# Gate logits and routing of a fused spectral-filter and mixture-of-experts kernel: transposes on VectorE in 32x32 blocks in place of TensorE's, and routing in a swapped order of columns

## The chip, the core and the metric

The kernel runs on one core of one Trainium2 chip. Its time is what the device needs for one execution, in microseconds (us). All arithmetic is in fp32. The engines are TensorE (PE in the profile, with PEld for its loads of the stationary operand), VectorE (DVE), ScalarE (ACT), GpSimd (POOL) and SyncE (SP, which issues most transfers). Each engine works its own instructions off in order and waits on semaphores for the others.

## The reference

Eight batches of 2496 tokens with 256 channels are filtered in the frequency domain along the tokens. Each filtered token then goes to the one of eight experts with the largest gate logit: two matrices, a relu between them, and the result times the softmax weight of that expert.

```
X = np.fft.rfft(x, axis=1)                    # x: (8, 2496, 256)
y = np.fft.irfft(X * (filt_r + 1j * filt_i), n=2496, axis=1)
y = y.reshape(19968, 256)
logits = y @ w_gate                           # (19968, 8)
expert_idx = argmax(logits); gate_w = softmax(logits)[expert_idx]
out = gate_w * (relu(y @ w1[e]) @ w2[e])      # w1: (8, 256, 1024), w2: (8, 1024, 256)
```

## The kernel before

**The filter.** A batch of 2496 = 39 x 64 tokens is transformed by matrix products in four stages, `stage_a` to `stage_d` (L342 to L412). Stages a and b are the forward transform over 39 and over 64 points, stages c and d go back. Between a and b, and between c and d, the data goes through DRAM (`zd`, `ud`) and comes back in another layout; the first batch stays in the chip and is turned by transposes on TensorE instead. `stage_d` writes y into tiles `yo`, 117 tokens (three groups of 39) to a partition column: 22 columns a batch, in six chunks of at most four, `CH`. Each chunk's `yo` is one of six buffers (`YB`).

**The logits.** `turn_y` transposes a chunk on TensorE against the identity, 117x128 at a time, so that the channels lie on the partitions (L482), and copies the result from PSUM to the tile `yt` (four buffers). `logits` multiplies `yt` by the gate matrix, two halves of 128 channels, with four column tiles of 32 side by side (L496); `ls` takes the result out of PSUM. `turn_logits` transposes it back on TensorE (L507) and copies it to `lgs`, so that tokens lie on partitions again. Every such copy goes through `evac`, whose line in the profile is L234 and which gives it to DVE or ACT by the planner's own count of how busy they are.

**The routing.** `route` (L514 to L599) handles a group of two chunks, up to eight columns: DVE finds the largest logit and the expert. Two matmuls count the tokens ahead of each one within its expert (L554 with the triangle `tri`, L555 with `ones`), a scan adds the counts of earlier columns, and out comes the row that each token takes in the list of its expert. GpSimd writes the token's number and weight behind its 256 channels and scatters the rows to DRAM, one column of 117 rows to an instruction (L615). Only when a chunk's rows are scattered may its `yo` be written again.

**The experts.** Tiles of 512, 256 or 128 rows of one expert are read back, transposed on DVE (L748) and go through the first matrix (L791 for most tiles, with seven products of quarters in place of eight; L832 for the others), the relu, and the second (L849). The results are scattered to the output (L855).

**The order.** PE, DVE, ACT and SP follow an order that is written by a planner while the program is built. `slot(k)` lists the steps of batch k's middle stages, of the next batch's first and of the previous batch's last stage with its logits and routing, each with a place in the slot and a cost in us of TensorE time. A running clock `now` adds these costs; expert steps are put between the filter steps as soon as the planner believes that their rows and weights are there. Instructions of `route` are handed out a few at a time after each step, from a list `sides` of which only the first entry moves.

Of the kernel before, what the change touches and what calls it, by code (L numbers as in the profile page):

```python
# [19 lines left out]
P = 128  # L20
S = 2496
D = 256
# [16 lines left out]
FT = F // P  # L39

# [13 lines left out]
def dft_tables():  # L54

    w = 2.0 * np.pi  # L60
    q = np.arange(N1)
    t = np.arange(N2)

    ta = np.zeros((NB, N1, NB, NS))
    td = np.zeros((NB, NS, NB, N1))
    for f in range(NF):
        ang = w * ((q * f) % N1) / N1
        for j in range(NB):
            ta[j, :, j, f] = np.cos(ang)
            td[j, f, j] = (2.0 if f else 1.0) / S * np.cos(ang)  # L70
            if f:
                ta[j, :, j, NF + f] = -np.sin(ang)
                td[j, NF + f, j] = -2.0 / S * np.sin(ang)

    ang = w * ((t[:, None] * t[None, :]) % N2) / N2
    c, sn = np.cos(ang), np.sin(ang)
    tb = np.block([[c, -sn], [sn, c]])
    tc = np.block([[c, sn], [-sn, c]])

    ids = np.zeros((NB, N1, NG))  # L80
    valid = np.zeros((NB, N1, NG))
    for j in range(NB):
        for i in range(len(range(j, N2, NB))):
            ids[j, :, i] = token(q, NB * i + j)
            valid[j, :, i] = 1.0


    sg = np.where(coefficients() <= S // 2, 1.0, -1.0)

    return {  # L90
        "ta": ta.reshape(TP, TK),
        "tb": tb,
        "tc": tc,
        "td": td.reshape(TK, TP),
        "sg": np.concatenate([sg[:, :NF // 2], sg[:, NF // 2:]]),
        "ids": ids.reshape(TP, NG),
        "valid": valid.reshape(TP, NG),
    }
# [22 lines left out]
def kernel(  # L121
# [65 lines left out]
    tds = cst.tile([TK, TP], F32, name="tds")  # L187
# [4 lines left out]
    CT = 32  # L192
    wg = cst.tile([P, DH, CT], F32, name="wg")
    tri = cst.tile([TP, TP], F32, name="tri")
    ones = cst.tile([TP, P], F32, name="ones")

    WM = 8
# [4 lines left out]
    vld = cst.tile([TP, NG], F32, name="vld")  # L202
# [63 lines left out]
    def load_rest():  # L266
        nc.sync.dma_start(out=tds, in_=td)
        nc.vector.memset(wg, 0.0)
        nc.sync.dma_start(out=wg[:, :, :E], in_=moe_w_gate.rearrange("(i p) e -> p i e", p=P))
        nc.sync.dma_start(out=ids0, in_=ids)  # L270
        nc.sync.dma_start(out=vld, in_=valid)

    def make_constants():
        make_identity(nc, ident)
        nc.gpsimd.memset(ones, 1.0)
        nc.gpsimd.affine_select(
            out=tri, in_=ones[:, :TP], compare_op=ALU.is_gt, fill=0.0, base=0, pattern=[[1, TP]], channel_multiplier=-1
        )
        nc.gpsimd.memset(seg, 1.0)
        nc.gpsimd.memset(seg[:, :, 0:1], 0.0)  # L280
        nc.gpsimd.memset(tot, 0.0)
        nc.gpsimd.iota(prow, pattern=[[0, 1]], base=0, channel_multiplier=1)
        nc.gpsimd.iota(tau_i, pattern=[[1, 64]], base=0, channel_multiplier=0)
        nc.vector.tensor_copy(tau0, tau_i)
        nc.gpsimd.iota(e_i, pattern=[[1, E]], base=0, channel_multiplier=0)
        nc.vector.tensor_scalar(em8, in0=e_i, scalar1=-float(E), scalar2=None, op0=ALU.add)
        nc.vector.tensor_scalar(eoff, in0=e_i, scalar1=float(TE), scalar2=None, op0=ALU.mult)
        nc.vector.tensor_copy(cnt, eoff)
        nc.vector.tensor_copy(done, eoff[0:1, :])
        nc.vector.memset(one, 1.0)  # L290
# [10 lines left out]
    ins, outs, lgs, yts, lands = {}, {}, {}, {}, {}  # L301
# [95 lines left out]
    def stage_d(b, c):  # L397
        if c == 0:
            lgs[b] = sb.tile([TP, NG, E], F32, tag="lg", name="lg")
# [3 lines left out]
        yo = outs["o", b, c] = sb.tile([P, 4, DR], F32, tag="y", name="yo", bufs=YB)[:TP]  # L403
        for j in range(0, n, 2):
            p = bank()
            if i0 + j + 2 < NG:
                mm(p[:TP, :], lhsT=tds, rhs=ui[:TK, j:j + 2, :], start=True, stop=True)
            else:

                for i, k in enumerate((TK, NS)):  # L410
                    mm(p[:TP, i * D:(i + 1) * D], lhsT=tds[:k, :], rhs=ui[:k, j + i, :], start=True, stop=True)
            evac(yo[:, j:j + 2, :D], p[:TP, :].rearrange("p (i d) -> p i d", i=2), 512)  # L412
# [63 lines left out]
    def turn_y(b, c):  # L476
        yo = outs["o", b, c]
        for j in range(0, CH[c][1], 2):
            pt = bank().rearrange("p (i q) -> p i q", i=4)
            for i in range(2):  # L480
                for dh in range(DH):
                    nc.tensor.transpose(  # L482
                        pt[:, 2 * i + dh, :TP], yo[:, j + i, dh * P:(dh + 1) * P], ident[:TP, :TP]
                    )
            yt = yts[b, c, j] = sb.tile([P, 4, TP], F32, tag="yt", name="yt", bufs=4)
            evac(yt, pt[:, :, :TP], 4 * TP)

    def logits(b, g):

        js = range(min(4, NG // 2 - 4 * g))  # L490
        w = len(js) * CT
        pair = [yts.pop((b, 2 * g + j // 2, 2 * (j % 2))).rearrange("p (i h) q -> p i h q", i=2) for j in js]
        lt = psr.tile([P, 2, E * NG], F32, tag="lt", name="lt")[:, :, :TP]
        for dh in range(DH):
            for j in js:
                mm(lt[j * CT:(j + 1) * CT], lhsT=wg[:, dh, :], rhs=pair[j][:, :, dh, :],  # L496
                   start=(dh == 0), stop=(dh == DH - 1))
        ls = sb.tile([P, 2, TP], F32, tag="ls", name="ls", bufs=1)
        evac(ls[:w], lt[:w], 2 * TP)
        outs["l", b] = (g, w, ls)  # L500

    def turn_logits(b):
        g, w, ls = outs.pop(("l", b))
        n = w // CT
        pt = bank()[:TP, :2 * w].rearrange("p (i w) -> p i w", i=2)
        for i in range(2):
            nc.tensor.transpose(pt[:, i, :], ls[:w, i, :], ident[:w, :w])  # L507
        evac(lgs[b][:, 8 * g:8 * g + 2 * n, :].rearrange("p (j i) e -> p i j e", i=2),
             pt.rearrange("p i (j c) -> p i j c", c=CT)[:, :, :, :E], 16 * n)

# [3 lines left out]
    def route(b, c0, c1):  # L514

        t0 = 4 * c0
        w = min(4 * c1, NG) - t0
        lg = lgs[b][:, t0:t0 + w]
        sh3 = (TP, w, E)
        she = (TP, E, w)  # L520

        def small(name, *shape, dt=F32, tag=None):
            n = int(np.prod(shape))
            full = sb.tile([TP, WM * n // w], dt, tag=tag or name, name=name, bufs=1)[:, :n]
# [10 lines left out]
        nc.vector.tensor_tensor(oh, oh, em8[:TP, None, :].to_broadcast(sh3), op=ALU.mult)  # L535
# [3 lines left out]
        if t0 + w == NG:  # L539

            nc.vector.tensor_tensor(idx, idx, vld[:, t0:t0 + w], op=ALU.mult)
        oe = small("oe", E, w)
        nc.vector.tensor_tensor(
            oe, idx[:, None, :].to_broadcast(she), em8[:TP, :, None].to_broadcast(she), op=ALU.is_equal
# [9 lines left out]
        mm(rk[:TP, 0, :E * w], lhsT=tri, rhs=oef, start=True, stop=True)  # L554
        mm(rk[:, 1, :E * w], lhsT=ones, rhs=oef, start=True, stop=True)  # L555
        pos = small("pos", E, w, tag="oh")
        nc.scalar.copy(out=pos.rearrange("p e t -> p (e t)"), in_=rk[:TP, 0, :E * w])
# [3 lines left out]
        sd = small("sd", w)  # L561
# [7 lines left out]
        nc.vector.tensor_tensor(pos, pos, tot[:TP, :, :w], op=ALU.add)  # L569
        yield 2  # L570
        nc.vector.tensor_tensor(pos, pos, oe, op=ALU.mult)
        row = sb.tile([TP, WM], U32, tag="row", name="row", bufs=2)[:, :w]
        rowf = small("rowf", w)
        nc.vector.tensor_reduce(rowf, pos.rearrange("p e t -> p t e"), axis=AX.X, op=ALU.add)
        yield 2
        nc.vector.tensor_copy(row, rowf)
        nc.vector.tensor_copy(cnt, tot[:, :, w])
        yield 2
        for i, yo in enumerate(yos):
            n = min(4, w - 4 * i)  # L580
            sh8 = (TP, n, 8)
            nc.gpsimd.tensor_scalar(
                yo.bitcast(I32)[:, :n, D:D + 8], in0=ids0[:, t0 + 4 * i:t0 + 4 * i + n, None].to_broadcast(sh8),
                scalar1=float(b * S), scalar2=None, op0=ALU.add,
            )
            nc.gpsimd.tensor_copy(yo[:, :n, D + 8:], sd[:, 4 * i:4 * i + n, None].to_broadcast(sh8))
        free["p"] = max(free["p"], now[0]) + 0.5 * len(yos)
        rows = []
        for t in range(w):
# [3 lines left out]
        for t, (at, what) in enumerate(rows):  # L593
            scatter(b, at, what)
            yield "pool"
            if t % 4 == 3 or t == w - 1:
                held_y[0] -= 1
        if t0 + w == NG:
# [268 lines left out]
    def slot(k):  # L867
# [22 lines left out]
        if k > 0:  # L890
            for c in range(nch + 3):
# [5 lines left out]
                if c >= 3 and c % 2:  # L897
                    steps.append((at + 0.01, lambda c=c: logits(k - 1, (c - 3) // 2), None, 0.9, "d"))
                if 1 <= c <= nch:
                    steps.append((at + 0.03, lambda c=c: turn_y(k - 1, c - 1), None, 0.22 * CH[c - 1][1], "d"))  # L900
                if c >= 3 and c % 2:
                    later = at + (0.07 if k == 1 else 0.11)
                    steps.append((later, lambda c=c: turn_logits(k - 1), None, 0.25, "d"))
                    steps.append((later + 0.001, lambda c=c: sides.append(route(k - 1, c - 3, min(c - 1, nch))), None, 0.0, "d"))
# [251 lines left out]
```

## Time and profile before

| | |
|---|---|
| median of 14 runs | 1555.48 us (1549.07 to 1560.85) |
| the profiled execution, its own time | 1551.99 us |
| its span in the profile | 1550.3 us |
| mean granted TensorE clock | 0.984 |
| busy: PE, PEld, DVE, ACT, POOL | 1478.4, 1164.7, 750.6, 479.4, 697.3 us |
| bytes moved by DMA | 276.82 MB, 179 GB/s on average |

In the profile's lists a group of instructions has its line, engine, operation, the tile that is written and what is read, the shape of it as partitions x elements, the count and the busy time with the mean duration of one, and then the idle time of the engine just before these instructions. A matmul in fp32 leaves two records, a transpose one, each with a record of its weight load (LDWEIGHTS). Durations of matmuls contain the time until the last result is out, and consecutive ones overlap, so what a matmul costs in a stream is the distance between two starts, not its duration.

### The profile page before, as it was taken

To read this page: it belongs to the slowest core of one execution; us is meant where nothing else is said; L and a number is where in the kernel's file an instruction comes from. 1 tells how busy PE (TensorE), PEld (TensorE's weight loads), DVE (VectorE), ACT (ScalarE), POOL (GpSimd) and SP (SyncE) were. 2 spreads that over 40 slices of the span, in tenths; PEclk is the share of its full clock that TensorE was granted. 3 is DMA by queue.
4 is the path that set the end of the run, shared out by engine and by line. 5 is a ranking of instruction groups with operands and counts; after the bars stand their busy time and mean duration, and the time that the engine had idled before them with its cause. 6 is when DMAs were issued, how large, how long until landed. Compare 5 with 4: busy or idle time off the path is not lost. (4 is left out here: it accounts for less than half of the span.)

```text
span 1550.3 us, 23882 instructions
## 1 busy us (share of the span) xinstructions
PE 1478.4 (95%) x7202; PEld 1164.7 (75%) x7202; DVE 750.6 (48%) x1676; ACT 479.4 (31%) x993; POOL 697.3 (45%) x910
## 2 busy tenths in 40 slices
PE   7989897999999999999999998999999999999998
PEld 5543454776667886877778876788888889999997
DVE  4676475415754556555674555457443434440000
ACT  4444342233233233222332223222222222223333
POOL 4342244413625554445734545665455546641111
PEclk9998998999999999999999999999999999999999
DMA  9769898787686648835584565455556443455661
GB/s 235 209 178 294 239 295 239 223 223 235 201 246 165 181 132 241 200 106 157 142 220 114 138 156 130 134 153 155 174 155 192 148 142 107 122 185 170 178 187 40
DMA packets 215173, 276.82 MB, mean 179 GB/s; under 512 B 124227, under 2 KB 162508, under 8 KB 215045
## 3 DMA queue, kind: packets, MB, share of 16 engines
q1 hardware_dynamic: 195925, 231.94, 53.7%
q0 software_dynamic: 19120, 43.33, 8.3%
q8 instruction: 61, 1.00, 0.3%
q14 instruction: 67, 0.55, 0.1%
HBM read 195.19 MB, written 80.64 MB: 178 GB/s over the span
## 5 line engine op out<-in xcount | busy, mean ns | idle before, releaser
L795 DVE TENSOR_TENSOR hT<-bank,hT 128x512 f32<-128x512 f32 (+1 forms) x504 | 300.4, 627 | 322.0 <-PE bank L791 187.6
L849 PE MATMUL bank<-w2t,hT 128*128 128x256 f32 x1984 | 446.3, 383 | 6.2 <-ACT hT L799 3.5
L849 PEld LDWEIGHTS bank<-w2t,hT 128*128 128x128 f32 x1984 | 378.6, 192 | 73.2 <-issue 13.6
L855 POOL DMA_INDIRECT out_dram<-ys,ng x161 | 161.6, 1004 | 471.8 <-DMA out_dram<-ys,ng 112.5
L799 ACT ACTIVATE hT<-hT 128x1024 f32<-128x1024 f32 (+1 forms) x144 | 132.5, 956 | 322.2 <-DVE hT L795 318.7
L615 POOL DMA_INDIRECT rows<-yo,row x176 | 177.3, 1008 | 75.0 <-issue 54.1
L791 PE MATMUL bank<-xT,w1t 128*128 128x256 f32 (+1 forms) x864 | 193.2, 360 | 0.0
L854 ACT ACTIVATE ys<-bank,ng 128x256 f32<-128x256 f32 x137 | 64.9, 474 | 406.2 <-PE bank L849 303.2
L791 PEld LDWEIGHTS bank<-xT,w1t 128*128 128x128 f32 x864 | 153.3, 192 | 25.3 <-issue 7.2
L791 PE MATMUL bank<-sums,wsum 128*128 128x256 f32 (+1 forms) x576 | 135.8, 358 | 0.1
L849 PE MATMUL bank<-w2s,hT 128*128 x592 | 132.6, 379 | 0.0
L748 DVE STREAM_TRANSPOSE xT<-xg 128x512 f32<-128x512 f32 (+2 forms) x126 | 57.5, 494 | 146.0 <-PE bank L832 87.0
L832 PE MATMUL bank<-xT,w1t 128*128 128x128 f32 (+1 forms) x864 | 125.9, 301 | 1.9 <-DVE xT L748 1.8
L832 PEld LDWEIGHTS bank<-xT,w1t 128*128 128x128 f32 x864 | 115.1, 193 | 13.1 <-issue 7.6
L849 PEld LDWEIGHTS bank<-w2s,hT 128*128 128x128 f32 x592 | 110.3, 190 | 13.8
L791 PEld LDWEIGHTS bank<-sums,wsum 128*128 128x128 f32 x576 | 101.2, 191 | 20.9 <-issue 9.0
L369 DVE TENSOR_TENSOR ys<-bank,ht 128x512 f32<-128x512 f32 x80 | 55.0, 687 | 79.4 <-PE bank L362 74.7
L388 PE MATMUL bank<-ys,tcs 128*128 128x512 f32 x140 | 73.6, 609 | 10.1 <-DVE ys L378 7.0
L348 PE MATMUL bank<-fin,tas 117*120 117x512 f32 x154 | 76.5, 617 | 5.3 <-DMA fin<-in_x_dram 5.3
L766 POOL TENSOR_TENSOR wsum<-w1t 128x256 f32<-128x256 f32 x72 | 52.8, 734 | 60.8 <-PE bank L791 59.2
L362 PE MATMUL bank<-fin,tbs 128*128 128x512 f32 x140 | 75.0, 624 | 2.9 <-DMA fin<-zd 2.9
L838 ACT ACTIVATE hT<-bank 128x128 f32<-128x128 f32 (+1 forms) x206 | 61.2, 299 | 47.8 <-PE bank L832 39.4
(143 smaller groups left out, 1614.9 us busy)
## 6 DMA issues: line engine op xcount, KB each, us to landing
w1t<-in_moe_w_dram SPq DMA_DIRECT2D x126, 512.0 KB
w2t<-in_moe_w_dram SPq DMA_DIRECT2D x68, 512.0 KB
fin<-in_x_dram SPq DMA_DIRECT2D x39, 512.0 KB
fin<-zd SPq DMA_DIRECT2D x70, 256.0 KB
ud<-uo SPq DMA_DIRECT2D x70, 256.0 KB
zd<-zo SPq DMA_DIRECT2D x35, 480.0 KB
fin<-ud SPq DMA_DIRECT2D x35, 480.0 KB
xg<-rows SPq DMA_DIRECT2D x112, 128.0 KB
```

What stands on the lines that cost most here:

```text
L348: mm(p[:TK, :], lhsT=tas, rhs=xt[:TP, j:j + 2, :], start=True, stop=True)
L362: mm(p, lhsT=tbs, rhs=zi[:, j:j + 2, :], start=True, stop=True)
L388: mm(p, lhsT=tcs, rhs=ys, start=True, stop=True)
L615: sc = nc.gpsimd.indirect_dma_start(out=rowsd, out_offset=bass.IndirectOffsetOnAxis(ap=at, axis=0), in_=what, in_offset=None,)
L791: mm(q[:, v], lhsT=left[:, v * P:(v + 1) * P], rhs=right, start=True, stop=True)
L795: nc.vector.tensor_tensor(o, q, a, op=ALU.add)
L799: nc.scalar.activation(o.rearrange("p v r c -> p v (r c)"), q.rearrange("p v r c -> p v (r c)"), AF.Relu)
L832: mm(p[:, :m], lhsT=w1t[2 * i + g][:, dh, fh, v * P:(v + 1) * P], rhs=xts[i][:, dh, :m], start=(dh == 0), stop=(dh == DH - 1))
L838: lambda: nc.scalar.activation(hT, p[:, :m], AF.Relu))
L849: mm(p[:, :D], lhsT=hs[i][k % 4 // 2][:, k // 4, k % 2, j * P:(j + 1) * P], rhs=w2, start=(k == 0), stop=(k == FT - 1))
L854: lambda: nc.scalar.activation(ys, p[:, :D], AF.Copy, scale=gate))
L855: nc.gpsimd.indirect_dma_start(out=out, out_offset=bass.IndirectOffsetOnAxis(ap=gis[i].bitcast(U32)[:, j, :1], axis=0), in_=ys, in_offset= ...
```

## The change

The transposes of y and of the logits leave TensorE. `stage_d` now fills all 128 partitions of `yo` (its matrix `td` is padded with zero columns). `turn_y` is one DVE instruction for a chunk that transposes each 32x32 block of it where it stands, into the tile `ty`, of which there is one, for a group of two chunks. In a block the channels then lie on 32 partitions, once for each of the four blocks of 32 tokens on top of each other. The gate matrix is laid out to fit, as `wb`: eight pieces of 32 channels, each block-diagonal over the four blocks. `logits` is eight accumulating products for each of four column tiles, 64 columns each (for the last group of a batch, with six columns of tokens, 48 products). `turn_logits` is one DVE transpose of 32x32 blocks straight from PSUM.

This leaves the tokens of four columns in another order: block of partitions and column are swapped within a group. `route` counts in that order. At its end it forms `rx`, the row and weight under four masks, and four matmuls with the matrix `sel` (new L591 in the changed kernel) put them back in the order of the partitions. DVE then casts the rows and ACT copies the weights, and only then follow the two instructions of GpSimd and the scatters. Before the four matmuls the planner lets its clock pass DVE's by 1.0 us. All groups use the full width of eight columns. In the planner a `turn_y` step now costs 0, `logits` 1.5 in place of 0.9, and `turn_logits` 0.

```diff
 def stage_d(b, c):
-            mm(p[:TP, :], lhsT=tds, rhs=ui[:TK, j:j + 2, :], ...)
+            mm(p, lhsT=tds, rhs=ui[:TK, j:j + 2, :], ...)
...
 def turn_y(b, c):
-    for j in range(0, CH[c][1], 2):
-        for i in range(2):
-            for dh in range(DH):
-                nc.tensor.transpose(pt[:, 2 * i + dh, :TP], yo[:, j + i, dh * P:(dh + 1) * P], ident[:TP, :TP])
-        yt = yts[b, c, j] = sb.tile([P, 4, TP], F32, tag="yt", name="yt", bufs=4)
-        evac(yt, pt[:, :, :TP], 4 * TP)
+    if c % RC == 0:
+        outs["t", b] = sb.tile([P, WM, D], F32, tag="ty", name="ty", bufs=1)
+    nc.vector.transpose(
+        outs["t", b][:, 4 * (c % RC):4 * (c % RC) + n].rearrange("p i (j x) -> p i j x", x=CT),
+        outs["o", b, c][:, :n, :D].rearrange("p i (j x) -> p i j x", x=CT))
 def logits(b, g):
-    for dh in range(DH):
-        for j in js:
-            mm(lt[j * CT:(j + 1) * CT], lhsT=wg[:, dh, :], rhs=pair[j][:, :, dh, :], ...)
-    ls = sb.tile([P, 2, TP], F32, tag="ls", name="ls", bufs=1)
-    evac(ls[:w], lt[:w], 2 * TP)
+    whole = [(q, slice(0, RC if q + 4 * last < n else last), q) for q in range(4)]
+    again = [(q, slice(last, RC), q - 2) for q in range(4) if q + 4 * last >= n]
+    for parts in (whole, again):
+        for j in range(NJ):
+            for q, cs, of in parts:
+                mm(lt[q * CT:(q + 1) * CT, cs], lhsT=wb[:, j, :], rhs=ty[:, cs, of, j * CT:(j + 1) * CT], ...)
 def turn_logits(b, g):
-    for i in range(2):
-        nc.tensor.transpose(pt[:, i, :], ls[:w, i, :], ident[:w, :w])
-    evac(lgs[b]..., pt..., 16 * n)
+    nc.vector.transpose(lg, outs.pop(("l", b)).rearrange("p c x -> p (c x)"))
 def route(b, c0, c1):
...
-    nc.vector.tensor_copy(row, rowf)
+    nc.vector.tensor_tensor(rx, rs...to_broadcast((P, 4, 2 * w)), msk...to_broadcast((P, 4, 2 * w)), op=ALU.mult)
     nc.vector.tensor_copy(cnt, tot[:, :, w])
+    due = free["v"] + 1.0
+    while now[0] < due:
+        yield "wait"
+    for i in range(4):
+        mm(pr[i * CT:(i + 1) * CT]..., lhsT=sel, rhs=rv[:, i], start=True, stop=True)
+    nc.vector.tensor_copy(row.rearrange("p (c g) -> p g c", g=4), pr[:, :, 0])
+    nc.scalar.copy(out=gts.rearrange("p (c g) -> p g c", g=4), in_=pr[:, :, 1])
     for i, yo in enumerate(yos):
...
-            nc.gpsimd.tensor_copy(yo[:, :n, D + 8:], sd[...])
+            nc.gpsimd.tensor_copy(yo[:TP, :m, D + 8:], gts[...])
 def slot(k):
-    logits 0.9, turn_y 0.22 * CH[c - 1][1], turn_logits 0.25
+    logits 1.5, turn_y 0.0, turn_logits 0.0
```

## The prediction

> **What bounds the kernel now.** I read the page first: the busy line of TensorE, and the row of the clock that it was granted.
>
> ```profile
> PE 1478.4 (95%) x7202; PEld 1164.7 (75%) x7202; DVE 750.6 (48%) x1676; ACT 479.4 (31%) x993; POOL 697.3 (45%) x910
> ...
> PEclk9998998999999999999999999999999999999999
> ```
>
> TensorE is busy for 95% of the span, no other engine for half of it. To see where the other 5% and the slow clock lie, I asked for busy times by stretch; the columns are PE, PEld, DVE, ACT and POOL in us with their instructions, the clock, the share of the DMA engines and GB/s.
>
> ```profile
> 110.00:190.00 80.00, 66.21 (x228) 33.27 (x227) 45.57 (x113) 27.96 (x63) 25.48 (x33) 0.89 0.87 264
> 190.00:330.00 140.00, 127.91 (x527) 87.87 (x526) 73.11 (x218) 44.95 (x105) 59.50 (x75) 0.95 0.86 247
> ...
> 600.00:760.00 160.00, 158.43 (x728) 124.96 (x727) 86.67 (x170) 44.95 (x77) 72.92 (x94) 1.00 0.58 160
> ...
> 1030.00:1300.00 270.00, 269.68 (x1290) 237.90 (x1289) 119.94 (x239) 67.31 (x98) 141.65 (x183) 1.00 0.51 156
> ```
>
> From 600 us on TensorE never rests: a microsecond of its work that goes is a microsecond of time. From 110 to 330 us it rests for 26 us, and the clock falls to 0.89 and 0.95; there transfers (0.86 of the DMA engines) and hand-overs between engines matter too. So the change is costed as TensorE work, plus waits. The groups by line, shapes kept apart, name what it removes:
>
> ```profile
> L482 PE MATMUL bank<-ident,yo 117*128 117x117 f32 x352 | 43.8, 265 | 2.2 <-DVE yo L234 2.2
> L496 PE MATMUL lt<-yt,wg 128*32 128x234 f32 x352 | 27.5, 368 | 10.4 <-ACT yt L234 7.8 <-DVE yt L234 2.6
> L507 PE MATMUL bank<-ident,ls 128*117 128x128 f32 x32 | 6.1, 273 | 0.0
> L507 PE MATMUL bank<-ident,ls 96*117 96x96 f32 x16 | 3.2, 283 | 0.5 <-ACT ls L234 0.5
> ```
>
> **What it removes.** Durations overlap, so I take distances between starts, from the timeline of TensorE (start, length, what):
>
> ```profile
> 971.10 1.00 PE L496 MATMUL lt<-yt,wg 128*32 128x234 f32 x16
> 972.04 1.99 PE L791 MATMUL bank<-xT,w1t 128*128 128x256 f32 x8
> ...
> 975.60 0.96 PE L482 MATMUL bank<-ident,yo 117*128 117x117 f32 x8
> 976.40 1.04 PE L791 MATMUL bank<-sums,wsum 128*128 128x256 f32 x4
> ...
> 979.00 0.38 PE L507 MATMUL bank<-ident,ls 128*117 128x128 f32 x2
> 979.22 1.89 PE L791 MATMUL bank<-xT,w1t 128*128 128x256 f32 x8
> ```
>
> Eight transposes of y take 0.80 us, 0.100 each: 352 make 35.2 us. Two transposes of logits take 0.22: 48 make 5.2. A block of old logits takes 0.94 to the next start, and its first record starts 0.31 us after the record before it where 0.22 is usual: 1.03 us, and 24 blocks (three in each of eight batches) make 24.7. Together **65.1 us**. The Trainium skill (TensorE: Matmul & The Clock Gate, Part 4: PE-mode transpose) gives about 275 ns for a transpose within a kernel. That agrees with the 265 ns duration here, but not with the distance of 100 ns; by its figure the 352 would be worth 97 us, by this trace 35.
>
> **What it adds on TensorE.** The 16 records of an old block stand in four sets of four: within a set the starts lie 7 ns apart (the four column tiles run side by side), and set follows set after 198 ns for 234 columns, 0.85 ns a column. 4 x 0.198 = 0.79, so a block has 0.24 us on top, for getting into this mode of four tiles and out again. A new block has 32 products, so 64 records or 16 sets, of 64 columns each. The nearest rows for so few columns are the matmuls of the ranks:
>
> ```profile
> 84.50 0.32 PE L554 MATMUL bank<-oe,tri 117*117 117x64 f32 x2
> 84.66 0.39 PE L555 MATMUL bank<-oe,ones 117*128 117x64 f32 x2
> 84.89 0.65 PE L388 MATMUL bank<-ys,tcs 128*128 128x512 f32 x1
> ```
>
> Single records of L554 with 64 columns follow each other after 60 ns, those of L555 after 112 ns, which is what the loads of 128 weight columns allow; with 48 columns L554 shows 47. In the old blocks the four loads of 32 columns start 7 ns apart and delay all four tiles alike, by 27 ns (the first set takes 225 ns instead of 198), so the loads do not queue behind each other, and I take 60 ns a set. A block is 16 x 0.060 + 0.24 = 1.20 us; the last group of a batch has 16 more sets of 32 columns, taken at 47 ns: 1.95 us. 16 x 1.20 + 8 x 1.95 = 34.8 us. The four matmuls of the swap back are two such sets: 0.33 us, 24 times 8.0. Together **42.8 us**, net **-22.3**. Bounds: by columns alone (54 and 27 ns a set, 14 for the swap) 36.5 us, net -28.6; by 112 ns for every set 32.5 + 30.6 + 11.1 = 74.2, net +9.1. The trace has no set this short, hence the wide end. `stage_d` with 128 columns in place of 117 is free: L348 with 120, L407 with 117 and L362 with 128 weight columns all follow each other after 429 ns.
>
> A rule that speaks against the change: the Trainium skill (TensorE: Matmul & The Clock Gate, Part 1) says that starts of matmuls never lie less than about 25 ns apart. The 7 ns here is lower, but in bursts of four. If 25 ns held on average, by an estimate from that page a block would cost 64 x 0.025 + 0.24 = 1.84 us, the longer ones 2.64, and the net would be -6.6.
>
> **What moves to DVE.** The rows for transposes in 32x32 blocks:
>
> ```profile
> L748 DVE STREAM_TRANSPOSE xT<-xg 128x512 f32<-128x512 f32 x56 | 36.2, 685 | 0.3 <-issue 0.3
> ...
> L748 DVE STREAM_TRANSPOSE xT<-xg 128x128 f32<-128x128 f32 x42 | 10.6, 290 | 125.8 <-PE bank L832 67.1 <-DMA xg<-rows 45.7 <-DMA ng<-rows 6.5
> ```
>
> A chunk of 1024 elements is one line beyond these: 1.03 ns an element more, 1.22 us. 40 of these and 8 of 512 are 54 us; DVE loses the copies of `yt` that it had, 16 us, and ACT 33 us of `yt`, 7 of `ls`, 3 of logits. DVE goes from 48% to some 51%: this lies beside TensorE's work and costs nothing by its sum. Without that cover, in the worst case, 38 us. It costs where TensorE stands at a hand-over, and that is the next item.
>
> **Waits.** Gone are 10.4 us before L496, 2.2 before L482 and 0.5 before L507: 13.1. New ones I look for in the order of the changed program: for each logit block and each swap, how much TensorE work stands between the matmul that its chain hangs on and the block, against the DVE work of that chain. (1) In the batches of index 1 and 2 the blocks of the second and the third group stand back to back, and there is one `ty`: the two transposes of the third (1.22 + 0.69) can only start when the second has read it. With two hand-overs 2.3 us, twice: 4.6. (2) In the third batch the second group's transposes stand on DVE behind a copy of `yo` that waits for the scatters of an earlier chunk, and behind 31 small instructions of the tile map (some 0.16 us each): 6.9 us of DVE against 0.75 of TensorE, and perhaps 1 us for the scatter, 7. (3) Twice the swap follows the ranks with nothing between: ACT's three copies (0.21 + 0.22 + 0.22), DVE's scan, add, product and sum (0.35 + 0.31 + 0.31 + 0.27), `rx` as one more such (0.31), hand-overs 0.4: 2.6 each, 5.2. (4) Two later blocks lack 5.2 and 2.8. Sum 24.8, less 13.1: **+11.7**. Behind each such wait in PE's queue stand stage b, c and expert products, and then `evac` copies on DVE and ACT that wait for them. Bounds: -13.1 if none comes, +37 if it is twice as many, since the same count shows only some 1 us in the old order where the trace has 13.
>
> **Where the experts go.** The changed order has no expert product before the 40th matmul of stage b, and 14 us of them by the 45th; the old one has 84. In the trace of before, the time beyond plain TensorE work grows by 26 us from the 20th to the 40th, with 14 us of expert work in it, and by 20 us from the 40th to the 45th, with 71 in it. Filler did not prevent the loss, so I take nothing for its absence, between -10 and +15. The DVE transposes of rows, weights and gathers are the same number. Later routing by one round through TensorE delays GpSimd's scatters by some 2 us a group; from 600 us on expert tiles of earlier batches cover that.
>
> **Sum.** Against the profiled execution's own 1551.99 us: 1552.0 - 22.3 + 11.7 = 1541.4. The median of the runs is 3.5 us above that execution, so 1545.
>
> **Rivals.** *Waits eat the gain*, the one that ends slower. Between stage d and the scatters the change puts a transpose in DVE's queue, one `ty` and a second round through TensorE. A block on `yo` or `ty` holds DVE, and with it stage b. From 22 us above the waits now gone, thus from 35 us of new waits, it decides; at the upper bound of +37, and with +15 for the missing filler, it ends 30 us above before, 1585. For it: DVE is 57% busy from 110 to 190 us, and TensorE rests there already. Against it: from 600 us on the order has 2 us or more to spare at most places. *Loads bound the short sets*: 112 ns each, net +9.1, with the waits 1555.5 + 9.1 + 11.7 = 1576. Against it: the 27 ns for four loads. *New waits are no more than the old ones*: 1555.5 - 22.3 = 1533, or 1520 without any at all. That the change does not do what it says has no room: the order shows L482 and L507 gone.
>
> **How the numbers follow.** A difference under 0.2%, 3.1 us, can't be told from none with this kernel. Net gain with some of the waits (1523 to 1552): 0.55. Waits no more than the old ones, or none (below 1533 in part): 0.11. Waits eat the gain (1553 to 1585): 0.25. Loads bound: 0.09. Of the first, about 0.08 lies within 0.2% of before, and of the third 0.02. So faster 0.58, same 0.10, slower 0.32. The range leaves a tenth out at each end: 1519 to 1578; the likeliest case's own is 1523 to 1552.
>
> **What would show it.** In the profile after, a block of the new logits should take 1.1 to 1.2 us to the next start, with 54 to 60 ns from set to set; 2.0 us means loads. PE's busy time should fall by some 20 us, DVE's rise by some 35. The waits of PE on DVE's transposes and on `rx` should sum to some 25 us, nearly all before 600 us. The stretch up to 330 us should show no better clock. I am wrong if the blocks are as priced and the time does not fall: then the waits before 600 us have taken it.

## The result, and the profile after

The change made the kernel slower: 1592.09 us (median of 10 runs, 1584.23 to 1596.64) against 1554.6 us (47 runs by then), a ratio of 1.0231 with a 95% interval of 1.0211 to 1.0251. The profiled execution took 1588.95 us, its span is 1587.0 us against 1550.3. The busy line, the granted clock and the group of the new logits on the page of the changed kernel:

```profile
PE 1471.5 (93%) x8434; PEld 1158.4 (73%) x8434; DVE 788.7 (50%) x1739; ACT 447.6 (28%) x932; POOL 692.5 (44%) x917
...
PEclk9999897899999999999999999999999999999999
...
L508 PE MATMUL lt<-ty,wb 128*32 128x64 f32 (+1 forms) x1792 | 45.2, 241 | 48.4 <-DVE ty L491 30.0
```

TensorE's busy time falls by only 7 us, and 48 us of idle time stand before records of the new logits, 30 of them put down to `ty`. The same stretches of the span as before the change (PE, PEld, DVE, ACT, POOL in us, clock, DMA share, GB/s):

```profile
110.00:190.00 80.00, 66.35 (x378) 29.68 (x376) 60.61 (x137) 27.33 (x59) 16.46 (x23) 0.93 0.85 259
190.00:330.00 140.00, 100.20 (x546) 60.54 (x546) 78.56 (x211) 33.59 (x76) 46.52 (x64) 0.84 0.80 215
...
600.00:760.00 160.00, 152.87 (x847) 121.11 (x846) 90.27 (x178) 39.79 (x66) 77.22 (x100) 0.97 0.55 152
...
1030.00:1300.00 270.00, 268.10 (x1247) 234.39 (x1246) 132.08 (x257) 68.60 (x100) 144.85 (x190) 1.00 0.54 157
```

From 190 to 330 us TensorE works 28 us less than before (100.2 against 127.9), at a clock of 0.84 in place of 0.95. The waits of TensorE by what ended them (total, times, longest):

```profile
PE lt L508 <- DVE ty L491: 30.0, 7, 6.3
PE lt L508 <- issue: 18.5, 32, 1.2
PE bank L591 <- DVE cnt L582: 12.4, 4, 7.3
PE bank L360 <- DMA fin<-in_x_dram: 12.2, 2, 10.9
```

The first line is the hand-over on `ty`, the third the swap behind the ranks, both foreseen in kind. The second was not: 32 gaps of about half a microsecond, all but one in the middle of blocks, in which TensorE waited for nothing that the profile shows. On the timeline, such a block (start, length, in brackets the idle time before it):

```profile
99.49 0.86 PE L508 MATMUL lt<-ty,wb 128*32 128x64 f32 x43
100.57 0.26 PE L508 MATMUL lt<-ty,wb 128*32 128x64 f32 x3 [0.22 <-issue]
101.97 0.33 PE L508 MATMUL lt<-ty,wb 128*32 128x32 f32 x4 [1.13 <-issue]
103.39 0.27 PE L508 MATMUL lt<-ty,wb 128*32 128x64 f32 x4 [1.10 <-issue]
...
106.25 1.20 PE L508 MATMUL lt<-ty,wb 128*32 128x64 f32 x37 [0.44 <-issue]
```

43 records run at full pace, then one to four at a time, with 0.4 to 1.3 us from one start to the next (idle 0.2 to 1.1), as if instructions came late. I call this supply, as a name; what delays them no view shows.

**An account of TensorE.** For each record I took the distance to the next start, less what the same pair of records takes undisturbed, and summed what is over by what comes next. With the work removed and added, the sum gives the change of the span. Each row gives the value before and after, or the difference alone. The right column is from traces of before and after taken in the last three series, of which below. They are one execution each, on two chips, and the one of before took 1529.68 us, 5 us more than the median beside it (1524.39): the spans differ by 20 us where the medians of after_again's series differ by 29. So the right column accounts for two thirds of the loss.

| us | first traces | last series |
|---|---|---|
| transposes removed (priced at 0.100 and 0.110) | -40.4 | -40.4 |
| logit blocks, old to new | 24.1 to 39.7 | 23.5 to 35.1 |
| swap | +6.8 | +6.9 |
| gaps before a logit block | 0 to 24.4 | 0 to 26.9 |
| gaps inside logit blocks | 12.2 to 30.0 | 4.9 to 7.9 |
| gaps before the swap | 0 to 14.3 | 0 to 9.7 |
| gaps before stages a, b, c | 26.1 to 40.9 | 27.6 to 44.2 |
| gaps before ranks, transposes, experts | 40.7 to 22.2 | 31.8 to 15.8 |
| records at the lower clock | 19.0 to 22.0 | 12.3 to 14.3 |
| sum with small rows / change of the span | +36.8 / +36.7 | +20.2 / +20.1 |

Of the 30.0 us inside blocks 6.9 are two waits on `ty`, the other 23.1 are supply.

### The profile page after: what moved, and what is told of

Read it like the earlier page. It is cut to its first block, busy times and chain, and to the rows that moved or that the text cites. A ratio compares the mean times of both kernels' runs of the same rounds, so it can differ in the third digit from the quotient of the medians.

```text
span 1587.0 us, 26336 instructions
## 1 busy us (share of the span) xinstructions
PE 1471.5 (93%) x8434; PEld 1158.4 (73%) x8434; DVE 788.7 (50%) x1739; ACT 447.6 (28%) x932; POOL 692.5 (44%) x917
## 5 line engine op out<-in xcount | busy, mean ns | idle before, releaser
L868 PEld LDWEIGHTS bank<-w2s,hT 128*128 128x128 f32 x592 | 110.3, 190 | 13.8
L508 PE MATMUL lt<-ty,wb 128*32 128x64 f32 (+1 forms) x1792 | 45.2, 241 | 48.4 <-DVE ty L491 30.0
L360 PE MATMUL bank<-fin,tas 117*120 117x512 f32 x154 | 78.4, 631 | 12.2 <-DMA fin<-in_x_dram 12.2
L374 PE MATMUL bank<-fin,tbs 128*128 128x512 f32 x140 | 78.9, 655 | 4.6 <-DMA fin<-zd 4.2
L508 PEld LDWEIGHTS lt<-ty,wb 128*32 128x32 f32 x1792 | 36.7, 129 | 61.4 <-issue 34.3
```

What stands on the lines that cost most here:

```text
L360: mm(p[:TK, :], lhsT=tas, rhs=xt[:TP, j:j + 2, :], start=True, stop=True)
L374: mm(p, lhsT=tbs, rhs=zi[:, j:j + 2, :], start=True, stop=True)
L508: mm(lt[q * CT:(q + 1) * CT, cs], lhsT=wb[:, j, :], rhs=ty[:, cs, of, j * CT:(j + 1) * CT], start=(j == 0), stop=(j == NJ - 1))
L868: mm(p[:, :D], lhsT=hs[i][k % 4 // 2][:, k // 4, k % 2, j * P:(j + 1) * P], rhs=w2, start=(k == 0), stop=(k == FT - 1))
```

## Experiments

Two theories: **hand-over**, that the loss is waits on `ty` and behind it in the order, and **supply**, that it is the gaps inside blocks of many short records. A third, **filler**, says that expert products come too late to cover waits. Every ratio is to runs of the kernel before in the same series of runs on the same chip. In the first three series it took 1557 to 1561 us, in the last three, from wide on, 1523 to 1524. That is no matter of the chip alone, although some expectations call it one: one and the same chip gave 1557 us in the series of paced and 1524 in that of parted. What differs is not known.

**idle64** adds short records to the kernel before: 24 blocks of 32 unread products.

```diff
+        spare = bank()
+        for j in range(8):
+            for q in range(4):
+                mm(spare[q * CT:(q + 1) * CT, :64], lhsT=wg[:, j % 2, :], rhs=ht[:, 0, :64], start=(j == 0), stop=(j == 7))
```

> The kernel before, and nothing of the change, but behind each of its 24 blocks of logits stands a block of 32 products on four column tiles, 64 columns each, whose results nobody reads: the shape of the changed kernel's logits without its transposes and its swap. Undisturbed, such a block took 1.12 us of TensorE in the changed kernel, 24 of them 27 us. Supply theory (TensorE runs out of instructions where so many short ones stand together; the gaps of 0.6 to 1.4 us inside blocks, 23 us in the changed kernel's trace, depend on nothing else): such gaps appear here too, some 20 us, and the time is about 1555 + 27 + 20 = 1602. Hand-over theory (TensorE waits for VectorE's transposes and the swap, and the gaps are waits as well): no gaps in these blocks, about 1582.

1606.9 us, 1.0302 [1.0251, 1.0352]: 46 us for 27 us of work. One line of its waits of TensorE:

```profile
PE bank L501 <- issue: 25.9, 50, 1.2
```

The gaps come with the records, although nothing waits for a transpose here.

**idle256**: the same with 256 columns (`:64` becomes `:256`).

> The kernel before with the same 24 blocks of 32 unread four-tile products as idle64, but of 256 columns instead of 64: the same number of instructions, four times as slow a pace. By the pace of 0.85 ns a column a block takes 16 x 0.217 + 0.24 = 3.7 us, all 24 together 89 us. Theory of supply (short records are used up faster than instructions are fetched): at a record per 54 ns the fetch keeps up, the gaps inside the blocks that wait for nothing, 35 us in idle64, fall below 8 us, and the time is 89 to 97 us above before. Rival, that a block of four tiles stalls by itself however long its records are: gaps of 25 us or more remain, and the time is 115 us or more above before.

1652.26 us, 1.0594 [1.0545, 1.0643]. The time is as supply had it (92 us more for 89 of work), the gaps are not: 31 us inside the blocks, as against 35. So I had the threshold wrong: 49 ns a record is still faster than the few records per 0.65 to 1.3 us that come through between gaps. And six of ten rows of gaps begin within 14 records of each other in both: number 515 and 516 of all that TensorE executes, 943 and 945, 2152 and 2166, 2956 and 2954, 4802 and 4804, 5492 and 5494. Most go by the place in the program, not by the time at which it is reached.

**two_pieces**: two of the eight channel pieces of the logits (`range(NJ)` becomes `range(2)`).

> The changed kernel with two of the eight products in each sum of the logits: six pieces of 32 channels are left out, so a block has 8 products in place of 32 (12 in place of 48 in the last group), and all its waits stay where they are. By columns this takes 12 sets of some 0.056 us from each of 16 blocks and 24 smaller ones from 8, about 19 us in all. Supply theory: the gaps inside blocks, 23 us, go as well, and the time is about 1592 - 19 - 20 = 1553. Hand-over theory: the waits keep their size, about 1573.

1561.71 us, 1.001 [0.999, 1.0029]. The waits on `ty` stay, the second line of the changed kernel's list is gone:

```profile
PE lt L508 <- DVE ty L491: 35.0, 8, 6.5
...
PE bank L591 <- DVE cnt L582: 12.0, 3, 8.3
```

Of the 34 us won, 19 are work that is left out (blocks of 1.12 and 1.49 us become 0.45 and 0.48), so some 15 can be supply, not the 23 that the gaps sum to.

**no_turn**: y is turned for the first batch only, into a constant `ty`; the logits are of old rows.

```diff
+        outs["t", b] = outs["ty"]
+        if b:
+            return
```

> The changed kernel without VectorE's transposes of y after the first batch: the logits of batches 1 to 7 are formed from what the first batch left in the transposed tile. TensorE's instructions stay as many. Hand-over theory: the waits on the transposed tile, 31 us in the changed kernel's trace and nearly all after the first batch, go, and VectorE has 47 us less to do; about 1592 - 30 = 1562 or a little below. Supply theory alone: the gaps inside blocks stay, about 1585. Filler theory (the time is lost because the expert products start later, after the 35th product of stage b and not before the 30th): the order of the experts hardly changes here, so about 1588.

1559.63 us, 0.9998 [0.9973, 1.0023]: without the transposes 36 us go. As 48 us of transposes on DVE go with them (its busy time falls by 39), this run does not part the wait on `ty` from the load on DVE; paced, below, changes the order alone. Its supply gaps are still there:

```profile
PE lt L511 <- issue: 14.3, 24, 1.2
```

And its order has as few expert products ahead of the 45th matmul of stage b as the changed kernel (13.8 us, where before had 85; records counted). So their absence alone does not make the loss.

**no_swap**: before's `route` without the swap, rows in the order in which they come (tokens and rows do not match).

> The changed kernel with the routing of the kernel before: the swap of the order at its end (the masked copies, the four products, the second look at the planner's clock) is left out, and the tokens are routed by logits that stand in the swapped order. Hand-over theory: the waits before the swap, 14 us, and its 7 us on TensorE go, while the wait before the ranks comes back in part (11 us before, 3 after): about 1592 - 16 = 1576, and scatters come sooner. Supply theory alone: 1585. Filler theory: about 1588, since the experts start hardly earlier.

1610.38 us, 1.0299 [1.0251, 1.0348], slower than with the swap: a miss for each theory.

```profile
PE lt L507 <- issue: 47.5, 73, 1.9
PE lt L507 <- DVE ty L490: 23.3, 8, 10.3
```

The gaps of supply more than doubled with fewer instructions in the program: other blocks stand where the gaps fall. An edit elsewhere can change these gaps by some 30 us.

**both**: no_turn and two_pieces.

> no_turn and two_pieces in one kernel: y turned for the first batch only, and two of the eight channel pieces of the logits (the logits are of old rows and of a quarter of the channels). If waits on ty and gaps of supply are two separate losses, their gains add up: after's ratio of 1.023 less 0.023 less 0.022, 0.977 to 0.980 of before, some 1525 us. If they are one loss seen from two sides, the second brings little: 0.993 to 1.000.

1540.14 us, 0.988 [0.9844, 0.9915]: between the two expectations. TensorE has 46 us less work than before by the account (-40.4, -13.0 for the logits, +6.9 for the swap) and 20 are won; ranks and swap take over some of the waiting (14.5 and 16.8 us before them).

**late** plans the logit block and what follows later (one of its four moved steps):

```diff
-steps.append((at + 0.01, lambda g=g: logits(k - 1, g), None, 1.5, "d"))
+steps.append((at + 0.06, lambda g=g: logits(k - 1, g), None, 1.5, "d"))
```

> The changed kernel with the logit block planned later: at + 0.06 instead of + 0.01 of a round's length behind its stage d, the first chunk's transposes of the next group after it (0.065 instead of 0.03), routing 0.03 later. Nothing is left out, no instruction is added. Theory of the hand-over on ty: more TensorE work stands between the transposes and the block, the waits before and in L508 on ty (31 us) fall to 15 or less, those on rx (14 us) to under 8, and the time is 15 to 25 us below that of the changed kernel: ratio 1.007 to 1.014. Rival (the wait only moves, since rows reach the scatters and chunks of y come free later): ratio 1.020 to 1.027, with new waits at stages a, c or d. Supply gaps stay in both.

1589.09 us, 1.0189 [1.0151, 1.0227], between the two ranges. The waits moved, as the rival had it: 9.4 us on `ty`, but 17.3 on `lg`, that is, on DVE's turn of the block before in the one `lt`.

```profile
PE lt L508 <- DVE lg L513: 17.3, 4, 8.3
...
PE lt L508 <- DVE ty L491: 9.4, 1, 9.4
```

**spread** cuts each block into two halves (four pieces each, at + 0.035 and + 0.062).

> As late, but each logit block cut into two halves of four channel pieces, planned at + 0.035 and + 0.062, so that other matmuls stand between them wherever the plan has any. The same products; 0.24 us more for each block to get into four tiles and out again, 6 us at most. Theory of supply (only long rows of short records run out of instructions): gaps inside the blocks fall from some 23 to below 10 us, and the time is 8 to 15 us below late. Rival (the gaps go by the number of instructions): no less than late, up to 6 us above it.

1578.74 us, 1.0122 [1.0086, 1.0157], 10 us below late. Blocks with gaps of 0.4 us and more in a row fall from six to three, and supply inside blocks from 25 to 17 us, not below 10 as expected.

**paced** lets the planner hold a block back until DVE's modelled queue is through:

```diff
+        when["ty"] = free["v"] + 1.0        # in turn_y and turn_logits
-steps.append((at + 0.01, lambda g=g: logits(k - 1, g), None, 1.5, "d"))
+steps.append((at + 0.01, lambda g=g: logits(k - 1, g), "ty", 1.5, "d"))
```

> The changed kernel, nothing left out, no instruction added: the planner holds a logit block back until DVE's modelled queue has done the transposes it reads (and the turn of the block before), plus 1 us, and plans other matmuls first where there are any. In the order one of the two places with two blocks back to back is parted. Theory of the hand-over on ty: the waits in and before L508 on DVE fall from 54 us in all (24 before blocks, 30 inside, some 23 of them supply) by 10 to 20 us, and the ratio to before from 1.023 to 1.009 to 1.016. Rival, that DVE or the load of u is late whatever the order (as late showed, where the wait moved from ty to lt): 1.018 to 1.026. Supply gaps stay, in other blocks.

1573.42 us, 1.011 [1.0083, 1.0138]. In the account the gaps before the blocks fall from 24.4 to 3.7 us, and those inside grow from 30.0 to 44.2, by supply in other blocks and the pair that is still back to back. No matmul or transpose was added or left out.

**eased**: paced and spread in one, and the filler columns by one product.

> paced, with each block cut into two halves of four channel pieces that the planner keeps 1 us apart where it has other work, and the filler columns of the third group written with one product instead of eight (14 fewer products in each of eight batches). The outputs are the same. If supply (some 23 us) and hand-over (some 30 us) are what the change lost, and both go by the order alone: 23 x 0.8 less for supply, 10 to 20 less than after for waits, 3 for the filler columns, 6 more for entering four tiles once more per block: 25 to 38 us below the changed kernel, ratio 0.999 to 1.007. Rival, that the waits stay: 1.008 to 1.015.

1589.41 us, 1.0223 [1.0191, 1.0255], a miss: the blocks wait little now, the others more.

```profile
PE bank L360 <- DMA fin<-in_x_dram: 17.8, 4, 14.4
PE bank L597 <- DVE cnt L588: 13.7, 3, 7.8
PE lt L513 <- issue: 12.5, 16, 1.8
...
PE lt L513 <- DVE ty L491: 6.4, 3, 5.0
```

**wide** and **wide_paced** put the logits into one column tile: 16 records of 256 columns in place of 64.

```diff
+        for j in range(NJ):
+            mm(lt[:, :n], lhsT=wb[:, j, :], rhs=ty[:, :n, j * CT:(j + 1) * CT], start=(j == 0), stop=(j == NJ - 1))
```

> The changed kernel with its logits in one column tile: eight products of 256 columns (192 in the third group) for a block in place of 32 or 48 of 64 and 32, and four or six small transposes by DVE in place of one to bring them to the same place. Nothing is left out. 16 to 18 records a block in place of 64 or 96. By 0.85 ns a column a block takes 8 x 0.22 = 1.74 us, the third 1.31, together 38.3 us, against 29.8 that the blocks have without their gaps. Theory of supply: the gaps inside the blocks that wait for nothing (some 23 us) go, all but 2 us, the waits on ty stay; net 12 to 15 us below the changed kernel, ratio 1.012 to 1.016. Rival, that the gaps go with the place in the program and move to the instructions after the block (as in eased, where stages b and experts showed them): ratio 1.024 to 1.030.

> wide and paced in one: nothing is left out. paced stands at 1.011 with 44 us of gaps inside the blocks, of which some 13 are waits on ty and some 26 supply. If supply goes with the number of records, 26 less and 8.5 more for the columns: ratio 0.997 to 1.002. If supply gaps only move: 1.011 to 1.018.

1601.94 us, 1.0521 [1.0499, 1.0542], and 1564.34 us, 1.0277 [1.0254, 1.03]. My price was wrong (two records to a product), and before was faster in this series, so the changed kernel and paced were run beside them once more:

> The changed kernel itself, run beside paced, wide and wide_paced on one chip, since the kernel before took 1523 us on the chip where wide was timed and 1557 to 1561 on the three others. Ratio to before as at first, 1.021 to 1.025, if the loss does not depend on the chip.

> The kernel of paced. Theory of the hand-over: 17 to 21 us below after_again, as the two ratios 1.011 and 1.023 had it on different chips.

> The kernel of wide. My price for it was wrong: a product of fp32 is two records, so a block is 16 x 0.216 = 3.5 us and not 1.74, and the 24 blocks are 41 us more TensorE work than in the changed kernel (71 against 30). If the 23 us of gaps of supply go for good with the short records: 16 to 20 us above after_again. If they only move to other instructions: 36 to 42 above.

> The kernel of wide_paced, beside paced_again: 41 us more work, 26 us of gaps of supply less. If they go for good 13 to 17 us above paced_again, if they only move 36 to 42.

1553.08 us, 1.0212 [1.0174, 1.0251]; 1531.23 us, 1.0056 [1.0037, 1.0076]; 1597.96 us, 1.0483 [1.0455, 1.0511]; 1564.47 us, 1.027 [1.0246, 1.0295]. This was another chip, with before as fast as in the series of wide. The changed kernel loses as much, and here it has no gaps of supply. The block shown above, and the two largest waits, in after_again:

```profile
99.56 1.87 PE L508 MATMUL lt<-ty,wb 128*32 128x64 f32 x96
```

```profile
PE lt L508 <- DVE ty L491: 33.9, 8, 5.9
PE bank L360 <- DMA fin<-in_x_dram: 12.8, 2, 10.8
```

So wide had nothing to win, and its 45 us more (41 of work) say nothing about supply on the others. paced is 22 us below after_again by the medians and 17 by the spans of the two traces. The gaps before the logit blocks fall by 21 us (26.9 to 5.8), and the other rows together grow by 4. Its largest wait is less than half of after_again's:

```profile
PE lt L509 <- DVE ty L491: 15.3, 3, 9.6
```

**before_again** and **parted**, the last two, on a third chip, the one of paced, with before at 1524 us. parted never emits a late block:

```diff
-            elif f and ready(fs[n]):
+            elif f and ready(fs[n]) and not (n == 0 and f[2] == "ty" and late_in(f)):
```

> The kernel before once more, for its trace beside those of after_again and paced_again, in which the blocks of logits show no gaps of supply at all. If this chip is the fast one again (1523 us), its trace tells where it lost less there: the short records of the old logits and of the transposes (gaps of supply in the first trace that were not counted as such, 10 us or more), or the granted clock (0.992 against 0.984, some 10 us). On another chip: 1552 to 1562 us.

> paced with 2 us of slack instead of 1; a block that is late is not emitted even when the planner has nothing else ready, so that no two blocks stand back to back; and the filler columns of the third group by one product instead of eight. The outputs are the same. The waits before and in the blocks on ty, some 15 us in paced_again, fall below 5 us, and the filler columns give 3 to 4 us: 10 to 14 us below paced, ratio 0.996 to 1.000 on the fast chip, 1.000 to 1.005 on the others. Rival, that time lost between the stages of 110 to 330 us stays lost because the loads of that stretch are late: 1.003 to 1.010.

before_again took 1529.68 us. Against the first trace its account is lower before the ranks (11.9 to 3.4 us), in the old logit blocks (12.2 to 4.9) and at the lower clock (19.0 to 12.3). There were no gaps in short PE records to be saved, but idle time by "issue" falls on the engines that feed TensorE: ACT's from 110 to 76 us, DVE's from 23 to 0.3. So the kernel before may have paid for the same in the first series too, less visibly; that fits the ratio, which is the same in both, but was not tested.

parted took 1545.84 us, 1.0151 [1.0125, 1.0177], against 1.0056 for paced_again, a miss. The waits on `ty` are nearly gone and have come back elsewhere:

```profile
PE bank L360 <- DMA fin<-in_x_dram: 16.5, 5, 8.0
PE bank L594 <- DVE cnt L585: 13.8, 7, 5.5
...
PE lt L510 <- DVE ty L491: 4.8, 2, 2.5
```

No version that computes everything beats the kernel before; paced beats the changed one.

## Why the prediction was wrong

**The net of the work was priced right, in part by chance.** An undisturbed block takes 0.88 us from its first to its last start and 1.12 with the way in and out (predicted 1.1 to 1.2), set follows set after 56 ns (54 to 60), the swap takes 0.29 (0.33). The net of work was -22.3 in the sum; the account has -18.0 in the first traces, where some short records run slowly, and -21.9 in those of the last series. The longer third block of a batch was priced too high: 1.49 us where 1.95 was set, since its sets of two records follow each other after 32 ns and not 47. Undisturbed, the 24 blocks take 29.8 us and not 34.8; the account has 35.1, since in some blocks the records run slower. The rival *Loads bound the short sets* is out. DVE's busy time rose by 38 us as expected. PE's fell by 7 and not 20 in the first traces, where the new logits, broken up by gaps, count 45.2 us; in the last series they count 35.6, and PE's falls by 19.

The Trainium skill (TensorE: Matmul & The Clock Gate, Part 1) says that starts never come closer than about 25 ns. On four column tiles a block of 64 records takes 0.88 us here, 14 ns each on average, and the measurement decides.

**The step that failed is the sum of the waits, +11.7.** New waits were set at 24.8 us, and the old ones that go at 13.1. In the last series, free of supply, the new ones are 44.5 (26.9 before the blocks, 7.9 inside, 9.7 before the swap), and stages a, b and c, queued behind them, wait 16.6 more. Ranks, transposes, experts and old blocks wait 20.9 less. With 2.0 for the clock that makes +42, above the upper bound of 37. In the first traces the same rows make +55, of which 23 are supply; the 32 that are left lie inside the bound. Item by item in the first trace: (1) the two pairs back to back, 4.6 predicted, 6.9 measured; (2) the third batch's second group, 7 predicted, 6.3 measured, behind the tile map's small instructions as described (the copy of `yo` ahead of them waited for stage d, not for scatters); (3) the swap, 5.2 for two places, 14.3 at seven; (4) two later blocks with 8, where four waited 3.3 to 6.7 us each, 19 in all. So the count from the order found the kind and most of the early places, and missed the size: it counted where DVE's own work was longer than TensorE's, and took DVE as free when the chain began. DVE was not. Before the block at 370 us it stood for 7.2 us in front of a copy of `yo`, until scatters had read the buffer, and the transpose came only behind that and the tile map; before the one at 737 us it stood for 4.0 us in the routing, waiting for ACT:

```profile
361.71 0.69 DVE L240 COPY yo<-bank 128x512 f32<-128x512 f32 x1 [7.16 <-DMA rows<-yo,row]
...
368.94 1.24 DVE L491 STREAM_TRANSPOSE ty<-yo 128x1024 f32<-128x1024 f32 x1
```

```profile
734.00 0.22 DVE L565 TENSOR_REDUCE rs<-ex 128x8 f32<-128x64 f32 x1 [3.99 <-ACT ex L553]
```

**Two terms were not in the sum.** What stands behind a waiting block in PE's queue was named and not priced: stages a, b and c, +14.8 and +16.6 us. And supply: 23 us in the first trace. It was real in the first series, but does not decide: without it the ratio is 1.021, since the kernel before is faster as well.

**The rival that came true** is *Waits eat the gain*, with its mechanism and place. Its price of 1585 was short by 7, which is partly luck: it had 15 us for missing expert products, which no run shows as a cost, and no supply. The line "nearly all before 600 us" holds for the waits on `ty` only in part: 7.5 of their 30.0 us come later. For the loss it holds better: by 460 us both kernels have started 55 and 56 matmuls of stage b, but 136 and 105 us of expert products (140 and 110 in the last series; records counted, 0.216 us each).

**What stays open.** In every changed version TensorE works 15 to 37 us less from 110 to 330 us than before, and easing one wait (late, eased, parted) brought others. Whether the expert products missing there are only the result of the delay, or would have covered it, no run tells: none had before's order of experts. no_turn shows that parity is possible without them. Of its 36 us, paced gets some 20 by the order alone; whether the rest is the wait on `ty` or the load of the transposes on DVE was not parted. What stalls TensorE at certain places of the program was not found either.

## What to carry to other kernels

When a step moves from a full engine to one that is half busy, price the new hand-over first: find the stretch where the full engine already waits, and count what both engines have queued there, not the mean load. A single buffer between two engines wants its consumer held back in the plan until the producer's queue is through (paced, 20 us here), but easing one wait in a stretch short of other work mostly moves it. Compare variants in one series, with the kernel before beside them.

## What the runs showed of the hardware that was not expected

Bursts of short TensorE records can stall with no wait that the profile shows. In the first series, of 64 to 96 records at 14 ns each, 23 to 47 ran at pace and the next ones one to six at a time, mostly every 0.65 or 1.3 us, in seven of the 24 blocks of the first trace. That instructions come late is the likely reason; no view shows it. In idle64 and idle256, the same program at two paces, six of ten such places were the same within 14 records, so the short pace is not the condition: it happened at 49 ns a record too. In the last series the same program ran with none of these gaps (idle time of TensorE by "issue" 20.3 us against 0.4), and the kernel before was 2% faster; on one and the same chip the kernel before took 1557 and 1524 us, so the chip alone does not set it.
